# The order of 6,457 calls in an SSM and long-convolution kernel, written out anew

## The chip, the core and the metric

The kernel runs on one core of a Trainium2 chip. The metric is the device time of one execution in microseconds. The core has engines that run side by side, each with its own queue of instructions: PE (TensorE, matmuls, with PEld for its weight loads), DVE (VectorE), ACT (ScalarE), POOL (GpSimd) and SP (SyncE, which issues DMAs). An engine works through its queue in order, and an instruction that needs what another engine makes waits at the head of its queue, with all that stands behind it.

## The reference

Inputs are bf16, with a length of 2048, a width D of 448 and 256 modes per channel. Cut to what is computed:

```python
g = sigmoid((x * gate_w).sum(-1))
# branch A: a diagonal SSM; its kernel K has 2048 taps for each channel
P = exp(dt*A * l)                       # D x 256 x 2048, complex
K = einsum("dn,dnl,dn->dl", C, P, dt*B).real
a = irfft(rfft(x, 4096) * rfft(K, 4096))[:2048] + x * Dskip
# branch B: a shift of k by four taps, times v, then a convolution with ssm_k
kv = (four taps of k) * v
b = x * (irfft(rfft(kv, 4096) * rfft(ssm_k, 4096))[:2048] + kv * ssm_D)
out = g * a + (1 - g) * b
```

## The kernel before

The long convolutions are transforms in stages of matmuls. The 448 channels are cut into four quarters H (of each of 4 groups of 112 channels, 28); each of them is done for branch B and for branch A. A sequence is spread over frequencies by `spread` (matmuls with the table Wc into the PSUM tile ps_c), turned by `transform` (table W2, tile ps_2, which the profile calls ps), multiplied with the other factor's spectrum on DVE (`products`), and brought back by `stage_a` (table R, tile ps_a, result U) and `stage_b` (table G, tile ps_b). After each of these matmul groups the result is taken out of PSUM by a copy, nearly always on ACT ("evacuation"; CAST in the profile). There are three PSUM buffers for these groups. `swapped` makes a copy of a spectrum with its real and imaginary halves exchanged, by two DMAs (zsS<-zs).

The kernel K of branch A is made in eight blocks of 14 columns. `Tables.levels` and `Tables.reals` fill the table ET with powers: phases ks_ph on DVE, Sin and Exp on ACT (ACT has to load a table when it goes from one function set to another: ACT_TABLE_LOAD), products with magnitudes on DVE. `KGen.block` multiplies up two lists of powers, TQ (two buffers) and TP (one buffer), on DVE, and contracts them with up to 224 small matmuls into the one tile pk. ACT evacuates pk to kg_S, matmuls with a selection table gather it (ps_g) into kg_KT, and a spread brings it to zsK.

Other parts at the start: the tables Wc, W2, R and G are made from integer constants (POOL's iotas, small DVE operations in the tile scratch, Sin on ACT); the four taps of k are eight products kvt of DVE, summed by PE in ps_v with an identity matrix; the channel constants come from transposes ps_m of the loaded A, B and C ("modes"). The inputs are loaded by SP's queue. At the end, DVE weighs the last branch with the gate (tile ept), adds the rest (ug), and eight pairs of DMAs on SP and ACT store it.

The body is written once in program order, but nothing is issued there: `Order` only lists the calls (`Listed` stands in for each engine), 6,457 of them, numbered from 0. `Order.issue` then issues them as the string `ORDER` says, and ties each instruction to the one before it on its engine. The profile's line of nearly everything is L146 for that reason:

```python
for run in ORDER.split():
    a, _, b = run.partition("-")
    for f, args, kw in self.calls[int(a):int(b or a) + 1]:
        ins = f(*args, **kw)
```

A tile gets its buffer when it is first used in that order. The numbers that come up below:

| calls | what they are |
|---|---|
| 27 to 42; 43 to 48; 53 to 64 | SP's loads of k, of the modes, of v, ssm_k and u |
| 65, 73; 75, 74 | POOL's memset and iota; shift and identity made from it on DVE |
| 100, 110, 90, 120, 80, 130, 150, 140 | DVE: the products kvt, in the order of before |
| 234 to 241 | PE: transposes of one of the modes |
| 1463 | DVE: product that overwrites a spectrum, behind the DMA that reads it for its exchanged copy |
| 3996, 3997 | ACT Sin into ET; DVE product with its magnitude |
| 5398, 5399 | DVE: the two halves of a phase ks_ph |
| 5421, 5422; 5430, 5435, 5439 and 5431 | the same pairs for the last chunk of ET |
| 5446 to 5461 | ACT: the 16 Exp of the last chunk |
| 3681; 4427, 4428; 5196, 5197 | DVE: products of 128x3584, 2.02 us each |
| 3758, 3775, 3792 | ACT: evacuations of U from ps_a |
| 5084, 5125; 4810 | ACT: evacuations of a gather (kg_KT); of a transform |
| 5492; 5493 to 5716 | DVE: the last of block 6's TP; PE: its pk |
| 5879; 5880 to 6103 | DVE: the last of block 7's TP; PE: its pk, 224 matmuls |
| 5809 to 5824, 5827 to 5842 | PE: transform of zsK's first half (quarter 3), ps_2 |
| 5845 to 5848, 6271 to 6274 | DVE: products of 128x896 with the halves of zsK |
| 6105 to 6121, 6123 to 6162 | PE: the two gathers of block 7 |
| 5198 to 5256 | PE: ps_a groups (stage a of quarter 2) |
| 6164 to 6192; 6178, 6193 | PE: spread of block 7; its evacuations on ACT and DVE |
| 6205 to 6238 | PE: transform of zsK's second half |
| 6201, 6202 | DVE: the last mix of branches (uu, ug) |
| 6304; 6305 to 6452 | DVE: last evacuation of U; last stage b and its epilogue |

Of the kernel before, what the change touches and what calls it, by code (L numbers as in the profile page):

```python
# [41 lines left out]
    "604 23 166 27 73 65 26 31 576 1 75 164 525 74 24 36 76 171 194 192 172-173 198 193 25 35 188 177 174-175 195 582 "  # L42
    "189 580 176 0 34 199 581 201 162 593 160 33 163 594 161 190 165 595 588 167 2 168 577 32 597 178 169 606 602 29 "
    "22 16 191 17 179 21 12 38 13-14 18-19 15 181 186 10 28 180 182 8 170 20 9 3 187 6 183 37 11 7 5 4 30 536 534 528 "
    "526 184 42 79 68 529 185 527 46 535 39 537 544 47 542 196 545 531 197 44 550 202 200 590 583 552 45 543 541 584 "
    "596 589 48 585 591 100 40 530 41 55 533 43 586 101-108 592 603 587 72 67 599 598 49 110 51-52 538 66 90 50 56 "
    "234-241 69 77 532 54 120 53 109 64 242 70 63 215-222 78 80 539 62 243-250 71 540 225-232 61 223 549 224 233 "
    "121-128 130 548 203 546 204 131-138 150 129 547 111-118 551 139-140 600 151-158 119 553 601 554 251 141-148 159 "
    "557 252-259 267 149 319-326 260 327 302-317 556 285-300 318 261 91-98 301 262 555 205-212 81-88 213 99 214 263 "
    "268-283 264 89 265 1110 284 266 574 367 474 346-353 575 366 1111 472 578 471 481 1108 365 354 1109 476 502 473 "  # L50
    "607 364 470 469 468 475 494 561 579 570 565 573 558 566 559 517 563 516 569 478 518 490 512 503 507 498 477 513 "
    "487 489 479 482 519 491 608-635 493 480 483 492 495 486 484 387-402 488 499 496 500 508 1126 522 497 501 485 521 "
    "504 524 370-385 523 514 2488 505 509 636-663 515 506 510 664-691 520 1124 511 1113 692-719 386 1127 1115 1114 "
    "1116 560 421-428 1122 1117 1120 567 403 1129 1119 562 820-835 1131 571-572 1118 720 568 1112 564 429 1852 1121 "
    "721 803-818 2495 2510 2489 2499 2491 1133 2493-2494 2496 1123 2492 722 2490 1135 337-344 836 57 60 59 58 723 "
    "1125 2497 1141 404-419 819 724 345 725 355-362 2511 2498 1137 420 786-801 605 1128 363 777-784 1138 802 328-335 "
    "1130 1140 785 743-758 336 1132 430-437 1142 759-775 1134 1143 438 1464-1479 776 1136 457-464 1851 1139 1853 2500 "
    "1272-1335 1854 1862 837-844 1855 1857 1336-1367 465 1208-1271 2501 2503 2502 845 1856 2504 1480 369 368 2505 "
    "2520 1481-1496 2519 2512 1858 1515-1522 2521 960-967 1859 1144-1207 2506 2513 2523 1497 2514 2522 2515 1861 968 "
    "2524 448-455 1860 2516 439-446 1368 1864 1863 456 1369-1385 2517 2508 2507 2518 1865 969-976 1867 1386 447 1866 "  # L60
    "1387-1426 1869 977 1868 942-949 466 1427 726-741 950 1446-1451 2525 1498-1513 1870 742 2526 1848 1872 1514 1849 "
    "467 924-931 1847 932 906-913 1846 2509 1874 914 863-878 2542 2529 1877 2527-2528 897-904 2543 1523 1875 879-895 "
    "2545 1876 905 933-940 2530 2544 915-922 2563 896 2534 2531 2537 2562 2532 2538 1662-1669 923 2564 1850 2533 2565 "
    "941 1871 1644-1651 1670 1460 951-958 2566 1873 2535 846-861 1461 2569 1652 2536 1878 959 2202-2217 862 2568 1880 "
    "2218 978-1041 1879 2539 1452 1881 2555 2949-2964 1453-1458 2540 2074-2105 1463 2554 2556 2550 1043-1106 "
    "2557-2558 1462 2561 2546 2541 1882-1945 1459 2965 1107 2552-2553 2549 1042 2559 1437-1444 2551 1584-1599 2560 "
    "2573 1445 2567 2548 2966-2981 2547 1600 1428-1435 6194 3968 1618-1633 1436 2570 2982 1653-1660 2571 1946-2009 "
    "1661 2572 2574 1634 2010-2073 2577 3976 3994 3973 3988 1635-1642 3974 3987 3971 2576 2219-2234 2579 3975 2575 "
    "3977 3332 2581 1643 1601-1616 3995 3972 2583 3970 2106 2585 2578 1524-1539 2235 2588 2580 1617 3331 2125-2164 "
    "3333-3334 1575-1582 3969 2165 2582 1558-1573 1583 1540 3335 2107-2123 2584 1541-1556 1574 3337 1671-1678 2590 "  # L70
    "2124 2236-2251 1557 3338 2184-2189 1679 2589 1716-1779 2190 2199 3336 2252 2166-2173 2198 2591 3996 2983-2998 "
    "3339 1707-1714 1780 2174 3997 3000-3007 2999 3982 3341 2191-2196 3983 1715 2586 1698-1705 2197 2253-2260 3340 "
    "3008 3984 2587 1689-1696 1706 3343 2175-2182 2592 2261 1680-1687 1697 2322-2329 4008 3346 2785-2816 1688 "
    "2721-2784 4009 3348 2330 3985 3350 2183 2201 2593-2656 2200 2920-2927 2349-2356 2928 2657-2720 2357 3352 3354 "
    "3342 4010 2262-2277 3357 3345 2817 3344 4011 3989 3347 2818-2834 4012 2340-2347 4023 2278 4000 2313-2320 3999 "
    "4022 2348 3349 3156-3163 4024-4025 3351 2321 1781-1844 3164 4043 3353 4001 4014 2835 4013 2938-2945 4002 4015 "
    "3060-3067 3978-3979 2946 1845 2836-2875 3980 3043-3058 3990-3991 3068 3981 3992 4004 4016 2279-2294 3986 4003 "
    "3993 4005 4018 4042 2296-2311 3998 3355 3059 4044 3356 2295 2331-2338 3358 2312 3026-3041 4045 2876 3360 "
    "2929-2936 2339 2895-2900 4006 3361 4007 2909 3682-3697 2937 4017 4046 2910 4019 3359 2358-2421 4029 4047 "
    "3426-3489 4038 4020 4040 4050 4039 4037 2422 4021 4041 3362-3425 4030 4049 4031 3042 4048 3554-3585 4053 4052 "  # L80
    "4026 4034 4051 4032 4027 6197 4036 4033 2911-2918 4035 3490-3553 4028 4054 2919 5388 4057 3699-3714 3698 4812 "
    "2948 3733-3740 3586 3715 3138-3145 3741 2947 3129-3136 3146 3009-3024 5395 5390 3716-3731 5397 5402 5394 4056 "
    "5410 2901 5403 3025 4055 4059 2902-2907 4058 2908 4811 3174-3181 3732 4060 2886-2893 5411 4813 4062 5391 "
    "2423-2486 3137 4061 5393 5396 4064 5389 3811-3818 4063 2894 4069 3182 2877-2884 5392 2487 3069-3084 3819 4814 "
    "2885 3147-3154 3085 4070 3120-3127 3587-3603 3155 4815 3192-3199 4071 3604 4818 4446-4461 3200 4065 4820 "
    "3605-3644 5404 4068 4817 3103-3118 4066 3645 5399 3128 5398 3655-3662 4067 5400 3086-3101 5405 3663 4072 3119 "
    "3671-3676 5407 4265-4296 4816 3102 4732-4747 3677 5401 5412 4819 3802-3809 4748 5408 3646-3653 5414 4073-4136 "
    "4822 4821 5406 5413 4462 3678-3679 4823 3829-3836 4201-4264 5415 3654 4826 3837 6200 3165-3172 3664-3669 5416 "
    "4137-4200 4828 3810 5429 4830 3173 5428 5417 4832 5418 3183-3190 4824 4297 4825 4766-4773 4827 3191 3201-3264 "
    "4829 4774 3681 3670 5409 3820-3827 3265 5424 4298-4314 5423 4749-4764 3680 4315 5425 4463-4478 3828 4765 "  # L90
    "4316-4355 5426 4831 4409-4416 4479 3266-3329 5419 4833 4356 5420 4417 4839 5421 4838 5458 4480-4487 4382-4387 "
    "5422 4429-4444 4840 5457 5443 5427 5442 5459 5444-5445 3330 5463 5462 4835 4488 4391-4398 4388-4390 3793-3800 "
    "5455 5464 4836 4399 4357-4364 4834 5460 4841 4418-4425 5461 4445 4837 5473 5034-5065 5452 5465 5447 4842-4905 "
    "4426 6195 4970-5033 5448 5466 5454 5433 4365 5468 5456 5469 5451 5450 5467 5453 5446 5449 4375-4380 4400-4407 "
    "5430 5434 5470 4715-4730 6196 4906-4969 4408 5431 5437-5438 4731 5475 3759-3774 4428 4381 5066 5439 4366-4373 "
    "4802-4809 5476 5435 4427 4374 4810 5085-5124 5432 3776-3791 5125 5850 5472 3801 5471 3775 5067-5083 4549-4556 "
    "5436 5474 5084 4506-4521 5440 4557 5477-5478 5441 5151-5156 3742-3757 5479 3792 5480 5849 5482 5157 4567-4574 "
    "3758 5135-5142 5851 5484 4575 3838-3901 5486 4522 5490 5143 4540-4547 3902 4523-4538 5487 4548 5481 5144-5149 "
# [899 lines left out]
```

## Time and profile before

| what | us |
|---|---|
| median of 3 runs | 296.03 (294.1 to 296.98) |
| profiled execution | 296.28 |
| its span, first to last instruction | 293.9 |
| DVE idle in the span | 28.4 |
| ACT idle in the span | 39.6 |
| mean granted clock of PE | 0.874 |

The profile comes from one execution of the program. Its times count from the first instruction. A row of a timeline or a wait says in brackets how long the engine was idle before the instruction and what ended the wait. "Issue" is time in which an engine waited for nothing that the profile shows. The chain of waits is followed back from the last instruction to whatever released it.

### The profile page before, as it was taken

How to read it: one execution, taken by the hardware profiler on the slowest of the kernel's cores; microseconds unless marked ns; L12 is line 12 of the kernel's file. 1: busy time of each engine (PE TensorE's matmuls, PEld its weight loads, DVE VectorE, ACT ScalarE, POOL GpSimd, SP SyncE). 2: the span in 40 equal slices, each digit the busy share in tenths (PEclk: the TensorE clock that was granted, in tenths of full speed). 3: DMA queues.
4: the chain of work that ended last, by engine and by line, in shares of the span. 5: the costliest groups of instructions: out<-in, count | busy, mean ns of one | idle time of the engine just before them, and what ended most of it. 6: DMA issues, size and time to landing. Idle time of an engine off the chain costs nothing.

```text
span 293.9 us, 12044 instructions
## 1 busy us (share of the span) xinstructions
PE 214.2 (73%) x5387; PEld 186.9 (64%) x5387; DVE 265.5 (90%) x540; ACT 254.3 (87%) x411; POOL 9.4 (3%) x43
## 2 busy tenths in 40 slices
PE   0067771658866798997998688879687998689730
PEld 0043451547755688995888578769576897578730
DVE  8998999999999989898999999889999999795950
ACT  4999899999999998999799999989999997637500
POOL 7001100000000100000000000000000000000000
PEclk9995996755999895997999989989779999799965
DMA  7999999530234321023003310320500036000068
GB/s 129 189 189 150 164 156 265 104 58 0 46 85 65 62 68 49 4 51 79 4 2 65 76 41 3 64 68 6 125 4 2 4 79 161 19 6 4 2 113 141
DMA packets 53380, 21.34 MB, mean 73 GB/s; under 512 B 48720, under 2 KB 51664, under 8 KB 53328
## 3 DMA queue, kind: packets, MB, share of 16 engines
q1 hardware_dynamic: 48768, 19.42, 36.3%
q10 hardware_dynamic: 4560, 1.15, 2.3%
q8 instruction: 42, 0.69, 1.0%
q14 instruction: 10, 0.08, 0.1%
HBM read 10.01 MB, written 3.21 MB: 45 GB/s over the span
## 4 chain that ended last, share of the span: by engine, by line
ACT 49%; PE 20%; DVE 17%; issue 6%; SPq 2%; DMA 2%; DVEq 0%; ACTq 0%
ACT zs L146 15%; ACT ET L146 12%; ACT zsK L146 5%; PE ps_a L146 5%; ACT L146 4%; ACT U L146 4%; PE pk L146 4%; ACT ks_mag L146 3%; PE ps_b L146 3%; DVE kg_P L146 3%; PE ps L146 3%; PE ps_c L146 2%; SPq L146 2%; DVE kvt L146 2%; DVE zsS L146 2%
## 5 line engine op out<-in xcount | busy, mean ns | idle before, releaser
L146 ACT CAST zs<-ps 128x896 bf16<-128x896 f32 x48 | 44.7, 970 | 1.2 <-PE ps L146 1.2
L146 ACT CAST zs<-ps_c 128x1024 bf16<-128x1024 f32 (+1 forms) x48 | 44.1, 942 | 0.1
L146 PEld LDWEIGHTS <-s_W 128*128 128x128 bf16 x544 | 31.8, 106 | 16.7 <-issue 13.1
L146 PE MATMUL pk<-kg_TP,kg_TQ 128*25 128x32 bf16 x1792 | 32.5, 239 | 7.5 <-issue 7.2
L146 DVE TENSOR_TENSOR kg_P<-kg_TQ,ET 128x896 bf16<-128x896 bf16 (+2 forms) x56 | 36.4, 657 | 0.5
L146 PE MATMUL ps_a<-sa_R,zs 128*128 128x128 bf16 x224 | 34.3, 240 | 2.1 <-ACT zs L146 1.2
L146 PE MATMUL ps<-zs,s_W 128*128 128x112 bf16 x384 | 29.4, 228 | 7.4 <-ACT zs L146 5.7
L146 PEld LDWEIGHTS <-kg_TQ 128*25 128x25 bf16 x1792 | 28.1, 128 | 10.3 <-issue 8.5
L146 PE MATMUL ps_a<-sa_R,zsS 128*128 128x128 bf16 x224 | 33.6, 238 | 0.0
L146 PE MATMUL ps_b<-U,sb_G 128*128 128x28 bf16 x1024 | 28.3, 175 | 5.0 <-issue 2.0
L146 PEld LDWEIGHTS <-zsS 128*128 128x128 bf16 x224 | 30.2, 153 | 2.0 <-issue 1.7
L146 PEld LDWEIGHTS <-zs 128*128 128x128 bf16 x224 | 30.1, 152 | 1.9 <-DVE zs L146 0.5
L146 ACT CAST U<-ps_a 128x1024 bf16<-128x1024 f32 (+2 forms) x30 | 28.0, 964 | 3.8 <-PE ps_a L146 3.8
L146 PEld LDWEIGHTS <-sb_G 128*128 128x128 bf16 x1024 | 27.3, 96 | 6.0 <-issue 3.3
L146 DVE TENSOR_TENSOR kg_P<-kg_TP,ET 128x1792 bf16<-128x1792 bf16 (+1 forms) x32 | 31.0, 972 | 0.1
L146 PE MATMUL ps_v<-kvt,scratch 128*128 128x448 bf16 x64 | 16.1, 416 | 16.5 <-DVE kvt L146 14.1
L146 ACT ACTIVATE ET<-ks_ph 128x448 bf16<-128x448 int16 x40 | 23.2, 606 | 0.9 <-DVE kg_P L146 0.9
L146 DVE TENSOR_TENSOR kg_TQ<-kg_P 128x448 bf16<-128x448 bf16 (+2 forms) x56 | 23.5, 423 | 0.1
L146 PEld LDWEIGHTS <-scratch 128*128 128x128 bf16 x65 | 7.1, 112 | 24.0 <-issue 16.0
L146 PE MATMUL ps_c<-Wc,kv 128*64 128x128 bf16 x224 | 17.1, 310 | 7.1 <-ACT zs L146 6.5
L146 ACT CAST zsK<-ps_c 128x384 bf16<-128x384 f32 (+2 forms) x27 | 21.0, 779 | 0.2 <-PE ps_c L146 0.2
L146 DVE TENSOR_TENSOR kg_TP<-kg_P 128x896 bf16<-128x896 bf16 (+2 forms) x40 | 20.3, 507 | 0.9 <-PE pk L146 0.9
(103 smaller groups left out, 456.8 us busy)
## 6 DMA issues: line engine op xcount, KB each, us to landing
zsS<-zs SPq DMA_DIRECT2D x16, 448.0 KB, 5.4
kt<-in_B_k_dram SPq DMA_DIRECT2D x16, 112.0 KB, 4.1
vt<-in_B_v_dram SPq DMA_DIRECT2D x4, 448.0 KB, 6.9
skraw<-in_B_ssm_k_dram SPq DMA_DIRECT2D x16, 112.0 KB, 3.4
uu<-in_A_u_dram SPq DMA_DIRECT2D x4, 448.0 KB, 9.1
xfd<-ks_hold SPq DMA_DIRECT2D x2, 672.0 KB, 4.9
ks_xf<-xfd SPq DMA_DIRECT2D x3, 336.0 KB, 3.1
out_dram<-ug SPq DMA_DIRECT2D x8, 112.0 KB, 4.4
```

The lines of the kernel that those rows point to most:

```text
L146: ins = f(*args, **kw)
```

## The change

The calls, tiles and buffers are the same; the string `ORDER` is another permutation of the same 6,457 numbers. Every engine's order changes: the instructions of PE, DVE, ACT and POOL and the DMAs that SP and ACT issue. In the large it follows the same course. The 512 DVE calls up to call 5879 and its set are the same ones in both, in another order. On PE, 16 matmuls (5809 to 5824) go from ahead of pk of block 7 to behind it. On ACT, the Exps 5453, 5450 and 5449 go behind the last three Sins, which makes one more change of function set. On SP the loads at the start change places, the DMAs of an exchanged copy change within their pairs, and of the stores at the end the chunks come in another order. The lines of the string with the calls named above, of both orders:

```diff
--- before.py
+++ after.py
@@ -39,73 +39,74 @@
 NBH = 1
 
 ORDER = (
-    "604 23 166 27 73 65 26 31 576 1 75 164 525 74 24 36 76 171 194 192 172-173 198 193 25 35 188 177 174-175 195 582 "
...
-    "121-128 130 548 203 546 204 131-138 150 129 547 111-118 551 139-140 600 151-158 119 553 601 554 251 141-148 159 "
...
-    "2218 978-1041 1879 2539 1452 1881 2555 2949-2964 1453-1458 2540 2074-2105 1463 2554 2556 2550 1043-1106 "
...
-    "3339 1707-1714 1780 2174 3997 3000-3007 2999 3982 3341 2191-2196 3983 1715 2586 1698-1705 2197 2253-2260 3340 "
...
-    "3605-3644 5404 4068 4817 3103-3118 4066 3645 5399 3128 5398 3655-3662 4067 5400 3086-3101 5405 3663 4072 3119 "
...
-    "4426 6195 4970-5033 5448 5466 5454 5433 4365 5468 5456 5469 5451 5450 5467 5453 5446 5449 4375-4380 4400-4407 "
-    "5430 5434 5470 4715-4730 6196 4906-4969 4408 5431 5437-5438 4731 5475 3759-3774 4428 4381 5066 5439 4366-4373 "
...
-    "5436 5474 5084 4506-4521 5440 4557 5477-5478 5441 5151-5156 3742-3757 5479 3792 5480 5849 5482 5157 4567-4574 "
...
-    "5489 4576-4583 4539 3903-3966 5483 4584 5491 5485 5150 5492 4558-4565 3967 4784-4791 5126-5133 5852 4566 "
...
-    "5791 5876 5874 5792-5805 4714 5877 5169-5176 5806 5872 5878 5177 5809-5824 5875 5879 5826 5196 6072-6103 5825 "
-    "5944-6071 5197 5880-5943 6198-6199 5232-5247 6104-6121 5248 5807-5808 5846 5215-5230 5845 6122 5249-5256 5231 "
...
-    "5847-5848 6205-6220 6273 5322-5386 6222 6221 6274 6271 6241-6254 6272 5387 6201 6256-6269 6255 6202 6290-6303 "
...
+    "165 525 196 161 580 0 27 197 577 168 200 167 73 189 171 46 169 588 65 191 172 581 595 176 606 178 32 597 2 602 "
...
+    "531 52 56 90 533 53 70 540 54 215-222 62 120 109 67 77 539 71 225-232 64 78 223 63 538 111-118 224 61 150 233 "
...
+    "2557 2554 1453-1458 2558 2010-2073 2218 2966-2981 2556 2540 2549 1463 2949-2964 2561 2559 978-1041 2551 2555 "
...
+    "3000-3007 3995 2201 2657-2720 2348 3008 3996 4011 2313-2320 2817 3344 4000 3989 3999 2920-2927 3345 3997 4001 "
...
+    "4813 5392 5399 3147-3154 4814 3085 3120-3127 4066 2885 3103-3118 3155 4815 4067 3587-3603 3128 4820 3192-3199 "
...
+    "4399 4418-4425 4837 5467 5447 5034-5065 3792 4400-4407 5473 4970-5033 5470 4426 5469 3759-3774 4408 5437 6195 "
+    "5452 5446 5448 4428 5451 5430 4842-4905 3742-3757 4427 3775 4906-4969 3758 5433 4374 5431 5434 3838-3901 5432 "
+    "5438 5476 5435 5475 5850 5478 5439 5066 5472 4382-4387 5453 4540-4547 5480 5471 4523-4538 5436 5474 4388 5440 "
...
+    "5485 5491 4810 5490 4585-4648 5125 5852 5450 5449 5488 5151-5156 5853 4576-4583 4649 5492 5157 5855 5621-5684 "
...
+    "5944-6071 5197 5880-5943 6198-6199 5249-5256 6104 5232-5247 5257 5807-5808 6105-6121 5248 5198-5213 6122 "
+    "5215-5230 5214 6123-6162 5231 5827-5842 6163 5809-5824 5843 6179-6192 5844 5826 6193 6164-6177 5825 6178 "
...
+    "5258-5321 6255 6274 6273 6290-6303 5322 6275-6288 6201 6304 6289 6202 6343-6374 6305-6336 6375 6419-6450 6376 "
...
 )
```

## The prediction

> **What bounds the kernel now.** I read the busy row and the slices of the page first, then the sums by stretch, then the waits by engine, then the chain of waits in the tail, and last single rows of the timeline at the places where an engine idles.
>
> ```profile
> PE 214.2 (73%) x5387; PEld 186.9 (64%) x5387; DVE 265.5 (90%) x540; ACT 254.3 (87%) x411; POOL 9.4 (3%) x43
> 65.00:91.00 26.00, 20.58 (x535) 17.97 (x535) 25.83 (x62) 25.97 (x44) 0.00 (x0) 0.85 0.17 38
> 145.00:180.00 35.00, 28.61 (x745) 26.46 (x743) 34.50 (x74) 34.97 (x68) 0.00 (x0) 0.95 0.17 39
> 257.00:270.00 13.00, 10.96 (x413) 10.21 (x406) 8.76 (x9) 7.34 (x11) 0.00 (x0) 0.99 0.02 4
> 279.00:294.00 15.00, 3.10 (x122) 3.00 (x118) 4.07 (x8) 0.00 (x0) 0.00 (x0) 0.57 0.70 124
> ```
>
> The rows by stretch give the length, then PE, PEld, DVE, ACT and POOL busy. From 44 to 235 us DVE and ACT are both full: an order can move work there, but can only save an idle gap of both. After 255 us neither is full and the kernel is a chain of dependences; after 279 it drains to the store.
>
> No call is added or dropped, so durations stay and the whole question is idle time. DVE's last instruction before the tail is call 5879, the end of block 7's table of powers, which ends at 255.03. The same 512 DVE calls stand in front of it in both orders, 243.9 us of work, so 11.1 us are idle. These waits make up most of it, and ACT's own are as small:
>
> ```profile
> DVE kg_TP L146 <- PE pk L146: 1.8, 2, 0.9
> DVE kvt L146 <- PE ps_v L146: 0.9, 1, 0.9
> 106.86 2.02 DVE L146 TENSOR_TENSOR zs<-zs 128x3584 bf16<-128x3584 bf16 x1 [0.77 <-DMA zsS<-zs]
> 133.04 0.39 DVE L146 TENSOR_TENSOR ET<-ET,ks_mag 128x448 bf16<-128x448 bf16 x1 [0.86 <-ACT ET L146]
> 185.89 0.46 DVE L146 TENSOR_SCALAR ks_ph<-ks_xf 128x224 int32<-128x224 f32 x2 [0.75 <-ACT ET L146]
> 199.11 2.02 DVE L146 TENSOR_TENSOR zs<-zs 128x3584 bf16<-128x3584 bf16 x1 [0.36 <-ACT zs L146]
> 220.11 0.40 DVE L146 TENSOR_TENSOR ET<-ET,ks_mag 128x448 bf16<-128x448 bf16 x1 [0.63 <-ACT ET L146]
> 117.53 0.91 ACT L146 CAST zs<-ps 128x896 bf16<-128x896 f32 x1 [0.88 <-PE ps L146]
> 144.72 0.58 ACT L146 ACTIVATE ET<-ks_ph 128x448 bf16<-128x448 int16 x1 [0.88 <-DVE kg_P L146]
> ```
>
> **The method.** Every call is matched to its row by its place in its engine's order. For a call that waits on another engine I take its distance in the trace (its start less the producer's end), and add what the new order changes: busy time moved ahead of the waiting call, less busy time moved ahead of the producer. A gap goes if that sum is clearly positive; a wait comes, or grows, where it is negative.
>
> **The saturated stretch, to call 5879.** On DVE these gaps go: the tap product kvt at 27.96 (call 150 stands two products earlier, distance to its ACT evacuation still 1.2): 0.86. Call 3997 at 133.04 (2.36 to Sin 3996): 0.86. Call 1463 at 106.86, which waits for the swap DMA, has 3.0 us more DVE work ahead: 0.77. The phase 5399 at 185.89, now apart from its partner 5398: 0.75. Call 5431 at 220.11, now behind the two 2.02 us products 4428 and 4427 (1.89): 0.63. Call 3681 at 199.11 (0.39): 0.36. Sum 4.2 us. Waits that grow: the two on the single kg_TP buffer (0.55 and 0.32 more), its TQ partner 0.1, call 5422 behind Sin 5421 0.13, call 5492 behind Exp 5449 0.12; sum 1.2. DVE alone says -3.0 us.
>
> On ACT go 0.88 (117.53), 0.80 (142.13), 0.88 (144.72), 0.63 (32.87), 0.45 (31.34) and 0.32 (198.12): 4.0 us. But the new order makes one more table switch: Exp 5453 comes after the Sins 5430, 5435 and 5439, so after the run of Sin there is another of Exp, 14 loads for 13.
>
> ```profile
> 218.21 1.28 ACT L146 ACT_TABLE_LOAD   x1
> ```
>
> The first function behind such a load starts 1.31 us after the previous instruction ends (5430 at 219.50), so 1.3 us is the price. Here the Trainium skill speaks against the change: "ScalarE: Activation LUTs", section "What ACT_TABLE_LOAD costs", gives the same load but adds a drain, together about 2.66 us, and its rule is to do all calls of one set before switching. By the row ACT's sum is -4.0 + 1.3 = -2.7; by the rule -1.3. No row shows the drain, so I take 1.3.
>
> These sums are ceilings. The two engines feed each other, so a gap is saved only if both have the time, and ACT meets PE sooner in places: the three evacuations of U (calls 3792, 3775, 3758) were moved 8 to 13 us of ACT's work ahead, and against PE their distance becomes about -2 us if PE keeps its idle time (6.1 us between 205 and 235), nothing if PE's moved groups fill it. I take half of that, 1.1 us, as paid. So -2.7 + 1.1 = **-1.6 us at call 5879**, from -3.0 to +1.
>
> SP and POOL: the 16 loads of k, the six of A, B, C and the v and u loads change places in SP's queue. kvt 97, the first product, needs loads 31 to 34; the last is now eighth in the queue behind one 224 KB load, and eighth landed at 9.8; with about 1 us for the larger load it is 10.8. DVE gets there at about 13.6 (12.07 plus 1.6 us of small constants moved ahead): hidden, and about 3 us late before it costs. POOL's constants (iota 73 and memset 65) go behind the larger iotas, as the shift and identity that read them go later on DVE; PE starts at 14.13 anyway. The swap DMAs keep their order by pairs. The eight stores on each queue keep one per chunk.
>
> **The tail.** Rows:
>
> ```profile
> 253.93 1.10 DVE L146 TENSOR_TENSOR kg_TP<-kg_TP,ET 128x1792 bf16<-128x1792 bf16 x1
> 256.73 2.02 DVE L146 TENSOR_TENSOR zsS<-zsS,zsK 128x3584 bf16<-128x3584 bf16 x1 [1.70 <-ACT zsK L146]
> 255.97 0.91 PE ps L146 x16
> 256.87 2.56 PE pk L146 x135
> 259.43 1.37 issue
> 260.79 1.16 PE pk L146 x56
> ```
>
> (The last four are of the chain of waits: start, length, what.) Block 7's 224 matmuls could start at 255.1, but the transform 5809-5824 stands ahead of them and waits for ACT's zsK; they start at 256.80. The new order puts it behind: 1.7 us saved, and they end 5.25 us behind call 5879 instead of 6.92. Then it is given back. Two groups ps_a (0.67 and 1.23) stand ahead of the first gather and two of 1.23 ahead of the second, so the second gather ends 5.4 us behind pk, formerly 3.9. A DVE copy of 0.62 and the spread follow, which starts at about 11.75 behind 5879 (was 11.94). Behind it, ACT's zsK copy 6178 stands after four half copies (+0.5), the transforms 6205 and 6223 end 0.8 earlier, 1.2 us of products (5845, 5846) that filled a wait at 262.7 now lie in the busy part, and 6202 (1.09) leaves it, to run beside the last stage b. By rows the last stage b starts 11.55 behind the spread, formerly 11.70. Tail: **-0.3 us**, uncertain by 1.5. If the cover of 6202 fails (DVE late at the first addition) it costs up to its 1.09.
>
> **The issue waits.** PE waits 1.4 to 2.6 us "for nothing" in places such as 259.43. Counting matmuls, all six that are near 1 us or longer in pk, ps and ps_b without a late producer (at 166.41, 196.06, 216.94, 246.90, 252.27, 260.79) fall at numbers 128k+86 to 128k+88. The page's instruction queue moved 42 blocks of 16 KB in the span. The Trainium skill, "Runtime: NRT & Kernel Launch", section "Instruction fetch mechanics", says that code comes in blocks of 256 instructions (here 128 pairs of weight load and matmul), mostly hidden. The trace agrees on the spacing, not on the hiding. It matters because the boundary doesn't move with the order: number 4822 was the matmul 5881 of pk and is now 5897 of the same group. By the row I keep the 1.37 us in the tail; by the rule it would be gone and the forecast 1.4 lower. It is why no more than 1.7 is booked there.
>
> **The sum.** -1.6 - 0.3 = -1.9 on the profiled execution: 296.28 (its span 293.9 and 2.4 around it) to 294.4. It lies 0.25 above the median of 296.03; the runs spread from 294.1 to 296.98, more than the gain.
>
> **Rivals.**
>
> - *The gaps close fully* (0.25): DVE's -3.0 is reached and the U evacuations cost nothing, and a boundary misses pk: 296.3 - 3.0 - 0.3 - 1.4 = 291.6. For it: PE is idle 27% and the distances are positive. Against: the two kg_TP waits stay.
> - *A late Exp holds block 6* (0.20, slower). Exps 5450 and 5449 now stand on ACT behind two evacuations of gathers (5084, 5125) and a transform (4810); DVE's 5492, which ends block 6's TP, needs them, and pk of block 6 needs 5492. Distance -0.12 by busy time alone. It decides once PE brings the gather later than that: behind ACT are then all evacuations of U and zs, and a boundary wait (2.0 in the row of ps_b) on those gathers goes whole into the chain. Price 1.3 (load, now not covered) + 2.0 + 0.12, with none of the gains: 299.7.
> - *Nothing moves* (0.10): both engines full before and after, tail as worked out: 296.
>
> Forecast 0.45, its own range 293.0 to 296.2. About 1% is what a measurement of this kernel can tell from no change: below 293.1 is faster, above 299.0 slower. Faster: 0.25 of the first rival and 0.05 of the forecast; slower: 0.20. For 8 in 10 the range takes in most of the first rival and the lower half of the second: 290.6 to 299.2.
>
> **What would show it.** The waits of DVE for ACT ET and for the swap DMA shrink and those on pk stay near 1.8; 14 table loads; pk of block 7 starts within 0.3 us of call 5879, with the issue wait still in it; the second gather ends 5.4 us after pk. It would be wrong if call 5492 shows a wait for ACT of over 1 us, if ACT waits over 2 us for ps_a before 235, or if issue waits land on gathers in the tail.

## The result, and the profile after

| what | before | after |
|---|---|---|
| median of 20 runs each, us | 296.05 | 294.57 |
| lowest and highest, us | 294.1 and 298.34 | 291.22 and 298.04 |
| ratio to before, 95% interval | | 0.9925 [0.9895, 0.9954] |
| profiled execution and its span, us | 296.28, 293.9 | 294.42, 292.1 |

The kernel became 0.5 to 1.0% faster, 1.5 to 2 us; 294.4 was forecast. The ratios here and below leave out runs that are over 1.5% above the fastest of the same kernel, three of after's 20 and none of before's; over all 40 the ratio of the means is 0.9940. All lines of work are now L147, as `ORDER` is one line longer. The page's busy row of after:

```profile
PE 214.0 (73%) x5387; PEld 186.8 (64%) x5387; DVE 265.1 (91%) x540; ACT 255.3 (87%) x412; POOL 9.4 (3%) x43
```

The sums by stretch of after (length, then PE, PEld, DVE, ACT, POOL busy, the granted clock, DMA share, GB/s):

```profile
28.00:44.00 16.00, 12.80 (x119) 7.31 (x117) 13.11 (x15) 14.01 (x17) 1.83 (x1) 0.89 1.21 157
...
145.00:180.00 35.00, 29.02 (x766) 27.39 (x766) 34.93 (x72) 34.84 (x67) 0.00 (x0) 1.00 0.17 39
...
257.00:270.00 13.00, 11.82 (x319) 10.79 (x319) 6.64 (x11) 8.41 (x12) 0.00 (x0) 0.87 0.14 35
...
279.00:294.00 15.00, 1.52 (x59) 1.41 (x55) 3.19 (x7) 0.00 (x0) 0.00 (x0) 0.52 0.73 125
```

and the first of these stretches in the kernel before:

```profile
28.00:44.00 16.00, 12.97 (x128) 7.62 (x126) 15.34 (x16) 14.91 (x18) 1.93 (x1) 0.98 1.28 161
```

Work is the same to 1 us on every engine, so again only idle time has moved. The reader is to see three things: in this execution the front (28 to 44 us) got worse, DVE doing 2.2 us less work in it; the full stretches got a little fuller; and in the tail (257 to 270) PE's granted clock is 0.87 where it was 0.99. The waits of after (total us, times, longest) say where:

```profile
PE pk L147 <- issue: 4.3, 5, 1.4
ACT U L147 <- PE ps_a L147: 4.2, 4, 1.5
...
DVE ks_hold L147 <- PE ps_m L147: 2.9, 1, 2.9
...
DVE kg_TP L147 <- PE pk L147: 0.8, 1, 0.8
```

Single rows of after's timeline, first DVE, then ACT, then PE:

```profile
41.03 1.16 DVE L147 TENSOR_TENSOR ks_hold<-ps_m,ks_dt 128x448 f32<-128x448 bf16 x2 [2.86 <-PE ps_m L147]
...
222.98 1.28 ACT L147 ACT_TABLE_LOAD   x1
224.27 0.39 ACT L147 ACTIVATE ET<-ks_xf 128x224 bf16<-128x224 f32 x1
...
253.26 2.83 PE L147 MATMUL pk<-kg_TP,kg_TQ 128*25 128x32 bf16 x176 [1.85 <-DVE kg_TP L147]
257.54 0.92 PE L147 MATMUL pk<-kg_TP,kg_TQ 128*25 128x32 bf16 x48 [1.45 <-issue]
```

The course of the gain, as the end of a call in after less that in before: +1.1 us at call 264 (43.25; DVE, the front), +2.4 at call 1143 (78.08), -2.5 at call 3553 (165.98; PE), -1.8 at call 5879 (253.21), -1.5 at the last DVE instruction (282.69). So in these two executions the new order loses in the front, wins more than 4 us in the full stretches, gives some back before block 7, and gains nothing in the tail. How much of that belongs to the order and how much to the clock of the execution is a question to which the last experiments return.

### The profile page after: what moved, and what is told of

It is laid out like the page before. It is cut to its first block, busy times and chain, and to the rows that moved or that the text cites. A ratio compares the mean times of both kernels' runs of the same rounds, so it can differ in the third digit from the quotient of the medians.

```text
span 292.1 us, 12048 instructions
## 1 busy us (share of the span) xinstructions
PE 214.0 (73%) x5387; PEld 186.8 (64%) x5387; DVE 265.1 (91%) x540; ACT 255.3 (87%) x412; POOL 9.4 (3%) x43
## 3 DMA queue, kind: packets, MB, share of 16 engines
q10 hardware_dynamic: 4560, 1.15, 2.2%
## 5 line engine op out<-in xcount | busy, mean ns | idle before, releaser
L147 ACT CAST zs<-ps 128x896 bf16<-128x896 f32 x48 | 44.6, 955 | 0.8 <-PE ps L147 0.8
L147 ACT CAST zs<-ps_c 128x1024 bf16<-128x1024 f32 (+1 forms) x48 | 44.2, 946 | 0.1
L147 PEld LDWEIGHTS <-s_W 128*128 128x128 bf16 x544 | 31.7, 106 | 13.4 <-issue 9.8
L147 PE MATMUL pk<-kg_TP,kg_TQ 128*25 128x32 bf16 x1792 | 32.8, 239 | 7.2 <-issue 4.3
L147 DVE TENSOR_TENSOR kg_P<-kg_TQ,ET 128x896 bf16<-128x896 bf16 (+2 forms) x56 | 35.9, 650 | 0.2
L147 PE MATMUL ps<-zs,s_W 128*128 128x112 bf16 x384 | 29.0, 227 | 8.8 <-ACT zs L147 8.1
L147 PEld LDWEIGHTS <-kg_TQ 128*25 128x25 bf16 x1792 | 28.6, 128 | 9.9 <-issue 6.9
L147 PE MATMUL ps_a<-sa_R,zs 128*128 128x128 bf16 x224 | 33.6, 238 | 1.5 <-ACT U L147 0.7
L147 PE MATMUL ps_a<-sa_R,zsS 128*128 128x128 bf16 x224 | 32.8, 236 | 0.3 <-DVE zsS L147 0.3
L147 ACT CAST U<-ps_a 128x1024 bf16<-128x1024 f32 (+2 forms) x30 | 27.8, 952 | 4.4 <-PE ps_a L147 4.2
L147 DVE TENSOR_TENSOR kg_P<-kg_TP,ET 128x1792 bf16<-128x1792 bf16 (+1 forms) x32 | 30.8, 966 | 0.5 <-ACT ET L147 0.4
L147 PE MATMUL ps_b<-U,sb_G 128*128 128x28 bf16 x1024 | 28.2, 175 | 4.2 <-ACT U L147 2.0
L147 PEld LDWEIGHTS <-zsS 128*128 128x128 bf16 x224 | 30.0, 152 | 1.9 <-issue 1.2
L147 PEld LDWEIGHTS <-zs 128*128 128x128 bf16 x224 | 29.9, 152 | 1.6 <-DVE zs L147 0.3
L147 PEld LDWEIGHTS <-sb_G 128*128 128x128 bf16 x1024 | 27.7, 96 | 5.0 <-issue 3.1
L147 ACT ACTIVATE ET<-ks_ph 128x448 bf16<-128x448 int16 x40 | 23.4, 610 | 0.1
L147 DVE TENSOR_TENSOR kg_TQ<-kg_P 128x448 bf16<-128x448 bf16 (+2 forms) x56 | 23.2, 418 | 0.2
L147 PE MATMUL ps_v<-kvt,scratch 128*128 128x448 bf16 x64 | 17.6, 440 | 7.8 <-DVE kvt L147 6.0
L147 ACT CAST zsK<-ps_c 128x384 bf16<-128x384 f32 (+2 forms) x27 | 21.3, 795 | 1.3 <-PE ps_c L147 1.2
L147 PE MATMUL ps_c<-Wc,kv 128*64 128x128 bf16 x224 | 17.2, 307 | 5.4 <-ACT zs L147 4.6
L147 DVE TENSOR_TENSOR kg_TP<-kg_P 128x896 bf16<-128x896 bf16 (+2 forms) x40 | 20.0, 500 | 0.8 <-PE pk L147 0.8
```

## The experiments

Each kernel is the changed kernel with the edit shown. A list `CALLS` holds the numbers of `ORDER`, and `move(order, what, ahead_of)` puts some of them elsewhere. The ratio is to the kernel before on the same chip. The times within the span come from one profiled execution each, so a difference of 1 or 2 us between two rows need not come from the edit. e0 is the changed kernel with nothing moved, measured together with e3b, e4 and e5; over all 12 of its runs its mean is 0.9983 of before's. "In pk" is PE's wait without a visible cause in pk of block 7; the last column is the time from the end of call 5879 to the last DVE instruction.

| run | ratio, 95% interval | call 264 ends | call 5879 ends | in pk | tail |
|---|---|---|---|---|---|
| before | | 42.11 | 255.03 | 1.37 | 29.16 |
| after | 0.9925 [0.9895, 0.9954] | 43.25 | 253.21 | 1.45 | 29.48 |
| e0_control | 0.9964 [0.9933, 0.9994] | 42.91 | 254.39 | 1.14 | 29.36 |
| e1_front_new | 0.9907 [0.9869, 0.9944] | 43.03 | 254.25 | 1.35 | 29.02 |
| e2_tail_new | 1.0036 [1.0009, 1.0063] | 42.95 | 255.78 | 0.94 | 28.78 |
| e3_exp_early | 0.9922 [0.9891, 0.9952] | 41.59 | 251.63 | 1.79 | 29.95 |
| e3b_three_exps_early | 0.9926 [0.9896, 0.9956] | 41.59 | 250.84 | 3.13 | 31.25 |
| e4_gathers_first | 0.9958 [0.9922, 0.9993] | 41.68 | 251.86 | 3.19 | 32.30 |
| e5_shift_64 | 1.0103 [1.0068, 1.0138] | 41.58 | 254.03 | none | 30.29 |
| e6_evac_first | 0.9986 [0.9954, 1.0018] | 40.83 | 253.62 | 1.62 | 29.89 |
| e9_swap_late | 0.9886 [0.9846, 0.9927] | 41.59 | 250.74 | 0.91 | 28.01 |
| e10_old_tail_swap_late | 1.0008 [0.9978, 1.0038] | 41.58 | 250.69 | 1.00 | 31.68 |
| e11_gathers_swap_late | 0.9908 [0.9876, 0.994] | 41.58 | 250.94 | 1.14 | 29.73 |
| e12_fill | 0.9924 [0.9902, 0.9946] | 42.61 | 253.63 | 0.76 | 27.92 |

### Which half gains: the order up to pk, or the tail

```diff
+OTHER = numbers(BEFORE)
+FIRST = set(CALLS[:CALLS.index(6072)])
+CALLS = [i for i in CALLS if i in FIRST] + [i for i in OTHER if i not in FIRST]   # e1_front_new
+CALLS = [i for i in OTHER if i in FIRST] + [i for i in CALLS if i not in FIRST]   # e2_tail_new
```

> The new order up to the point where block 7's pk begins, and from there the order of before, with the transform 5809-5824 ahead of pk again. My theory: the gain is made in the saturated stretch, where call 5879 ends 1.8 us earlier, and the new tail is worth about nothing; so about 1.5 to 2.2 us under the kernel before, 294.0 to 294.6. The rival (starting pk at once is what gains, and the stretch ahead of it only shifts idle time): within 0.5 us of before, about 296.

> The order of before up to block 7's pk, and from there the new order: pk at once, the transform behind it. My theory: pk starts about 1.7 us earlier behind call 5879, the second gather ends later behind pk by about that, and the end is within 0.5 us of before, about 296. The rival (pk first is the gain): about 1.7 us under before, 294.3.

The new front with the old tail has the gain (0.9907, 2.7 us, more than the 1.5 to 2.2 expected); the old front with the new tail is 0.4% slower than before (1.0036), 0.8 to 1.1 us where within 0.5 was expected. So the gain is made ahead of pk, and the new tail by itself brings none in the times. In e2's profile the tail was 0.4 us shorter (28.78 for 29.16), and pk did start 0.2 us behind call 5879, for 1.8 in before; why its times are above before is not settled.

### The fourteenth table load

```diff
+CALLS = move(CALLS, [5453], 5430)               # e3_exp_early
+CALLS = move(CALLS, [5450, 5449, 5453], 5430)   # e3b_three_exps_early
```

> The new order with one call moved: Exp 5453 goes ahead of Sin 5430, so 13 table loads for 14. If the load is paid in full on the way to call 5879: 1.3 us faster than the changed kernel, 1.28 us less of ACT's busy time and call 5879 about 1 us earlier. If it lies in time in which ACT would have waited anyway: within 0.4 us of the changed kernel. If a load also drains the pipeline as the Trainium skill has it: 2.6 us faster.

This expectation rested on a slip: three Exps stand behind the Sins, and with one of them moved the load only went on to the next. The profile of e3 still has 14.

> The changed kernel with all three late Exps (5450, 5449, 5453) ahead of Sin 5430, so that the 14th table load really goes (the run with 5453 alone only moved it on to 233 us, since the other two stayed). If the load is paid in full: call 5879 about 1.3 us earlier and 1.3 us faster. If it is covered by ACT's waits for PE: within 0.4 us. If a drain belongs to it: 2.6 us faster.

Here it goes. The groups of instructions of e3b (busy us, mean ns, then idle time ahead):

```profile
L165 ACT ACT_TABLE_LOAD x13 | 16.7, 1283 | 4.2 <-DMA kt<-in_B_k_dram 4.0
```

Call 5879 ends at 250.84, against 251.86 in e4, whose order is that of after up to there and whose front was as early: 1.0 us. It is the wait of call 5492 for the late Exp 5449 that went. DVE's rows of 5492 in e0, and then in e3b:

```profile
236.84 1.09 DVE L165 TENSOR_TENSOR kg_TP<-kg_TP,ET 128x1792 bf16<-128x1792 bf16 x1 [1.14 <-ACT ET L165]
...
233.30 1.08 DVE L165 TENSOR_TENSOR kg_TP<-kg_TP,ET 128x1792 bf16<-128x1792 bf16 x1
```

In e4 that wait was 1.12 us, and 1.07 in e3, where the load stands right ahead of the late Exps. The edit takes away a load and brings the Exps forward at once, so the 1.0 us is what both are worth together; the load's part is not separated. No switch shows a drain: the next function starts 1.30 to 1.31 us after the instruction ahead of the load at every switch in before and after. The kernel is not faster than the control clear of noise (0.9926 against 0.9964, intervals overlapping), and in the tail of its profile the gain was lost: its timeline on PE has

```profile
250.89 2.88 PE L165 MATMUL pk<-kg_TP,kg_TQ 128*25 128x32 bf16 x176 [1.91 <-DVE kg_TP L165]
256.90 0.91 PE L165 MATMUL pk<-kg_TP,kg_TQ 128*25 128x32 bf16 x48 [3.13 <-issue]
```

### The waits for nothing that the profile shows

```diff
+            if n == 608:            # in PE's wait of 5.9 us for the gate's tile; overwritten later
+                jobs = [(self.tc.nc.tensor.matmul, (self.pg[:, 256:272],),
+                         dict(lhsT=self.R[:, 0:128], rhs=self.R[:, 0:16], start=True, stop=True))] * 64 + jobs
```

> The changed kernel with 64 matmuls more on PE, put where PE waits 5.9 us for the gate's tile (their result is overwritten), so that every later matmul's number is 64 higher. If the issue waits belong to fixed numbers (128k+86 to 128k+88): they all move to other instructions, at numbers that are 128k+22 to 128k+24 by the old count; the 1.45 us inside block 7's pk goes or moves by 64 matmuls, and the end comes 0 to 1.4 us earlier. If they belong to the instructions (the change of group, the PSUM tile, DVE or ACT traffic): they stay at matmul 4821 of the old count and the time is unchanged.

They belong to the numbers. Counted in its own stream, e5's waits lie at 128k+86 to 128k+90, as those of all other runs do (up to 128k+91 in before and e2), that is 64 matmuls earlier in the work. Its timeline shows pk of block 7 in one piece, and a wait later:

```profile
254.09 3.57 PE L169 MATMUL pk<-kg_TP,kg_TQ 128*25 128x32 bf16 x224 [1.13 <-DVE kg_TP L169]
...
260.99 0.28 PE L169 MATMUL ps_a<-sa_R,zs 128*128 128x128 bf16 x1 [1.53 <-issue]
```

The time was a miss: not 0 to 1.4 us earlier, but some 3 us later than the control (297.45 against 294.5). Its waits say why:

```profile
PE pk L169 <- issue: 6.7, 6, 2.1
DVE kg_TP L169 <- PE pk L169: 2.9, 3, 1.9
```

With the boundaries elsewhere, the pk groups of other blocks are hit harder, and DVE then waits for the single kg_TP. The same pair of rows fits part of the change's own gain: in before they were 7.2 and 1.8 us, in after 4.3 and 0.8. The prediction had left that out; how much of the gain it makes is not measured.

What a wait consists of can be read from the records of the instruction queue. In after PE takes matmul 4694 (the boundary ahead) at 253.98; a 16 KB packet runs from 254.62 to 256.07; PE goes on at 257.54. From passing one boundary to going on at the next it takes 3.1 to 3.6 us at this place in after, before, e0, e1 and e2, while 128 matmuls of pk take about 2.0 (224 of them took 3.57 us above). In e3b the packet starts 2.9 us behind the boundary (251.61, 254.53) instead of 0.6. Two rows by stretch show the DMA share in the 2.9 us from the boundary in e3b, and in the 2.9 us from the start of the packet in after:

```profile
251.60:254.50 2.90, 2.17 (x144) 2.01 (x133) 2.90 (x2) 0.00 (x0) 0.00 (x0) 1.00 0.84 168
```

```profile
254.60:257.50 2.90, 1.50 (x100) 1.37 (x90) 2.90 (x3) 0.00 (x0) 0.00 (x0) 1.00 1.02 228
```

What moves there is the last exchanged copy, 896 KB, issued by SP when its source and buffer come free: 5808 is issued by 252.13 in e3b and 254.55 in after, each about 0.6 us behind the boundary, and the copy moves in both stretches (DMA share 0.84 and 1.02). In before it had been issued by 246.36, far from this pk. The new order brings copy and fetch together. In after, e0, e1 and e6 the fetch starts beside the copy, 0.55 to 0.64 us behind the boundary, and the wait in pk is 1.1 to 1.6 us; in e3 it starts 1.51 behind, in e3b and e4 2.9, and the wait is 1.8 and 3.1 to 3.2. What decides between the two is open: the distance from copy to boundary is not it, as SP's second issue starts 0.08 us ahead of the boundary in e0 and e3b alike, and 0.11 in e6 and e4 alike. e9 takes the copy away from there:

```diff
+CALLS = move(CALLS, [5450, 5449, 5453], 5430)
+CALLS = move(CALLS, [6104, 5807, 5808], 6105)
 ...
+                if n in (5807, 5808):
+                    f = self.tc.nc.scalar.dma_start
```

> The changed kernel with the three Exps early (as before) and with the last exchanged copy's two DMAs (5807, 5808) issued by ACT behind 6104 instead of by SP, so that they move after block 7's pk and not during it. My theory (the fetch of the next 128 matmuls is asked for when PE enters a block, and stands behind the exchanged copy's 896 KB if that is already under way): PE's wait inside this pk falls from 3.13 us to 1.0 to 1.5 us, and the end comes about 1.7 us earlier than with the Exps alone. The rival (the long wait comes from where the pk stands in time, or from DVE and ACT): it stays near 3.1 us. If the copies then land too late, DVE's 5847 waits for them at about 267 us.

Its timeline, PE and then ACT's queue:

```profile
250.79 2.85 PE L168 MATMUL pk<-kg_TP,kg_TQ 128*25 128x32 bf16 x176 [1.50 <-DVE kg_TP L168]
254.55 0.92 PE L168 MATMUL pk<-kg_TP,kg_TQ 128*25 128x32 bf16 x48 [0.91 <-issue]
...
256.17 0.51 ACTq L168 DMA_DIRECT2D zsS<-zs  x1
256.71 0.61 ACTq L168 DMA_DIRECT2D zsS<-zs  x1
```

0.91 us for 3.13, and the copy comes in time for 5847 at 263.59. No profile without the copy near has a long wait: in the six whose copy is not near this pk (before, e2, e9 to e12) it is 0.76 to 1.37 us, in the seven where it is (after, e0, e1, e3, e3b, e4, e6) 1.14 to 3.19, in three of them over 1.7. With one profile for each kernel that fits the theory, and is not yet proof of it. (The move also puts 6104 on ACT behind the evacuation 5257, so ACT's copy of pk starts 1.2 us behind the end of pk.) The tail is 3.2 us shorter than in e3b, more than the 2.2 us of the wait. The rest goes with the clock: e3b has half clock from 257.0 to 260.4, e9 none there. With 0.9886, 291.52 us, e9 has the lowest ratio here: its interval lies below 1, and the ratio also below the changed kernel's (0.9925 and 0.9964 in two measurements; only the first of these intervals overlaps its own). Against e3b (0.9926) the intervals overlap, so the 1.7 us expected from the copy alone are not shown in the times.

### The tail's order

```diff
+TAIL = ("5232-5247 6104-6121 5248 5215-5230 6122 5249-5256 5231 6123-6162 5257 "
+        "5198-5213 6163 5214 6179-6193 6164-6178 5827-5844 5809-5826")
+CALLS = move(CALLS, numbers(TAIL), 5323)        # e4; e11 has e9's two moves besides
```

> The changed kernel with another order of the tail: only one group of ps_a ahead of block 7's first gather, the gathers as early as PE can take them, the transform 5809-5824 behind the spread. My theory (what the early start of pk gained is given back because the gathers wait behind two ps_a groups each): the second gather ends about 1.5 us earlier behind pk and the kernel ends about 1 us earlier than the changed kernel. The rival (the tail is bound by ACT's and DVE's copies and by the clock of PE there, so order doesn't matter): within 0.4 us of the changed kernel.

> The tail with the gathers first, now with the three Exps early and the exchanged copy late, so that the wait of 3.19 us in pk, which hid its effect, is out of the way. My theory (gathers behind two groups of ps_a each gave the early pk back): the wait is 1.0 to 1.5 us, the second gather ends about 1 us sooner behind pk than with the tail as changed, and the kernel ends about 0.5 to 1 us before the run with the copy late alone. The rival (copies on ACT and DVE and the half clock behind pk bound the tail): the same time within 0.4 us.

No gain is shown. From the end of pk to the end of the second gather it took 5.6 us in e4 (6.3 in e0), but the wait of 3.19 us ate that. In e11 that wait is gone, and the gather comes 5.1 us behind pk, just as in e9, and the ratio is above e9's (0.9908, intervals overlapping). Two things went against it: the issue of the copy's DMAs held ACT, and DVE's product 5848 waited for ACT's zsK, because I had put the transform 5809-5824 behind the spread (timeline of e11, ACT and then DVE):

```profile
256.03 2.85 ACTq L171 DMA_DIRECT2D zsS<-zs  x2
258.92 1.01 ACT L171 CAST U<-ps_a 128x1024 bf16<-128x1024 f32 x1 [2.44 <-PE ps_a L171]
...
265.18 0.63 DVE L171 TENSOR_TENSOR zs<-zs,zsK 128x896 bf16<-128x896 bf16 x1 [1.31 <-ACT zsK L171]
```

(The second row names PE, but its group of ps_a had ended by 257.1; ACT went on when the DMA issues were through.) So my theory that the gathers' place gave the early pk back is not supported; its effect with nothing else moved stays open.

> New order up to block 7's pk, the tail of before behind it, the three Exps early and the last exchanged copy late. If the parts add up: the new front with the old tail was 0.9907 of before, the Exps are worth about 1 us at call 5879, and the wait in pk stays near 1.3 us: about 0.987 of before, 291 us. If the old tail only gains because its DVE waits less, the Exps' gain is lost in the wait for the transform ahead of pk: about 0.990.

Its edit is e1's lines with e9's two moves. A miss (1.0008). The old tail had DVE's products 5846 and 5845 ahead of the gather's copy 6163, and the late copy now makes them wait (DVE timeline of e10):

```profile
262.16 0.63 DVE L241 TENSOR_TENSOR zs<-zs,zsK 128x896 bf16<-128x896 bf16 x1 [5.47 <-DMA zsS<-zs]
```

So e10 tests only this collision, not whether the parts add up.

### The wait in the front

```diff
+CALLS = move(CALLS, [556, 557, 554], 555)       # e6_evac_first
```

> The new order with three Sins of table G (554, 556, 557) moved on ACT behind the evacuations that follow them at 33 to 43 us. My theory: DVE's new wait of 2.86 us at 41.03 (ks_hold for the transposes ps_m, whose PSUM buffer ACT frees late) goes, and since DVE is 99% busy for the 200 us that follow, most of it reaches call 5879: 1.5 to 2 us faster than the changed kernel, about 292.8. The rival: the front is bound by ACT and PE as well, and the Sins come back as a wait of ACT or DVE before 110 us; within 0.5 us of the changed kernel.

No gain, as the rival had it: 0.9986, if anything slower than the changed kernel. DVE's wait at 41 us went (call 264 ends at 40.83), but the Sins come behind: ACT's first Exp (call 472) starts at 45.47, against 44.10 in e4, whose front ran at full clock as this one did, and DVE waits 1.15 us for ET at 53.63. Call 5879 ends at 253.62, not earlier than in after.

But e0, e1, e3, e3b and e4 have the front of after unchanged, and call 264 ends at 42.9 to 43.0 in the first two and at 41.6 to 41.7 in the others. Sums over two stretches of 3.41 us of after show the difference:

```profile
33.90:37.31 3.41, 1.68 (x41) 1.33 (x41) 3.38 (x4) 3.41 (x5) 0.00 (x0) 1.00 1.33 161
37.31:40.73 3.42, 3.42 (x15) 1.65 (x14) 0.85 (x1) 2.63 (x4) 0.00 (x0) 0.51 0.85 139
```

and of e4:

```profile
34.80:38.20 3.40, 1.91 (x29) 1.32 (x29) 3.37 (x3) 3.40 (x5) 0.00 (x0) 1.00 1.26 151
38.20:41.60 3.40, 3.30 (x37) 1.95 (x36) 2.39 (x6) 2.97 (x5) 0.00 (x0) 1.00 0.98 159
```

The same part of the work runs at half clock in after (0.51) and at full clock in e4. The clock records change only at steps of 3.41 us, whose phase differs from one execution to the next. I tabulated all such steps between 60 and 278 us of 13 profiles, by PE's busy share in one step and the clock granted in the next, where the step itself was at full clock (a step that lies on the edge of a class can fall to either side):

```
busy share   next at half clock   next at full clock
under 0.5            40                   0
0.5 to 0.6           14                  13
0.6 to 0.7           12                  51
0.7 to 0.8           11                 107
0.8 to 0.9            3                 148
over 0.9              0                 295
```

Under half and over 0.9 the share tells what comes; between 0.5 and 0.8 both outcomes occur, so it is not the whole rule. The changed front sits on the edge: a share of 0.49 in after, 0.52 in e0 (half clock follows), 0.56 in e4 (full). Where it falls under, call 264 is 1.3 to 1.7 us late and is not made up: call 5879 ends 1.4 us later in after than in e4, and 2.4 to 2.5 in e1 and e0, with the same order up to there. So the loss in the front was of that execution: at full clock the changed front brings call 264 to 41.6 us, before's to 42.11, and e2, with the front of before, ended it at 42.95. The tail is alike. Rows of after:

```profile
255.73:259.14 3.41, 1.96 (x84) 1.75 (x74) 3.38 (x3) 0.53 (x1) 0.00 (x0) 1.00 0.79 186
259.14:262.56 3.42, 3.42 (x44) 2.94 (x43) 0.07 (x1) 2.04 (x3) 0.00 (x0) 0.50 0.01 2
```

The wait of 1.45 us in pk makes the first step 57% busy, and the next, with the gathers in it, runs at half clock. In e9 the corresponding steps are fuller, and the clock stays at 1.00:

```profile
253.05:256.47 3.42, 2.51 (x105) 2.26 (x94) 3.38 (x3) 0.31 (x1) 0.00 (x0) 1.00 0.02 5
256.47:259.88 3.41, 3.32 (x60) 3.09 (x58) 0.27 (x1) 3.00 (x5) 0.00 (x0) 1.00 0.79 168
```

The last run tried to lift the front over the edge:

```diff
+FILL = {285: 20, 91: 20, 608: 88}   # matmuls of 64 columns ahead of these calls, overwritten later; on top of e9
```

> The run with the Exps early and the last exchanged copy late, plus 128 small matmuls whose result is overwritten: 20 ahead of the spread at 35 us and 20 ahead of the sum at 37 us, where PE waits 0.8 and 0.7 us, and 88 in PE's 5.9 us wait for the gate's tile; 128 in all, so that the block boundaries behind them stay where they are. My theory (the clock of each stretch of 3.41 us is halved when PE was busy less than about 55% of the stretch before; the changed kernel sits at 0.49 to 0.56 there, and where it falls under, the front is 1.7 us late and stays so to the end): PE's share there rises to 0.7 or more, call 264 ends at 41.6 us, no half clock begins at 37 to 38 us in any execution, and the times lose their upper part: 0.3 to 0.8 us less in the median than the same kernel without the fill (0.9886 of before), about 0.986. The rival (half clock in the front comes at random, or the extra matmuls only delay PE): the same or up to 1 us slower, with the same spread.

Partly right. The share rose to 0.66, not 0.7. Rows of e12:

```profile
34.80:38.20 3.40, 2.24 (x62) 1.99 (x62) 3.37 (x3) 3.40 (x5) 0.00 (x0) 1.00 1.32 160
38.20:41.60 3.40, 2.80 (x29) 1.68 (x26) 1.45 (x4) 2.44 (x4) 0.00 (x0) 1.00 0.93 151
41.60:45.00 3.40, 2.06 (x33) 1.35 (x32) 3.40 (x8) 2.32 (x3) 0.00 (x0) 1.00 1.34 156
45.00:48.45 3.45, 2.65 (x90) 2.53 (x87) 3.45 (x6) 3.44 (x9) 0.00 (x0) 1.00 1.42 178
```

and of e9 without the fill:

```profile
41.42:44.83 3.41, 0.56 (x8) 0.40 (x8) 3.41 (x7) 3.38 (x6) 0.00 (x0) 1.00 1.35 161
44.83:48.25 3.42, 0.00 (x0) 0.00 (x0) 3.42 (x5) 3.42 (x12) 0.00 (x0) 0.50 1.32 223
```

In e9 PE was busy 16% of the step from 41.4 us, and half clock followed, from 44.8 to 55.1; with the added work (which also makes the work behind it come later) it was busy 61% and 77% of the steps from 41.6 and 45.0, and the clock stays full until 51.8. So the clock followed a share that an edit had changed. The times lie closer (292.19 to 293.42, six runs; e9 290.66 to 292.97, six runs). But a group of 20 took 0.75 us, as long as the wait it was to fill, and held up what came behind: the sum after it starts at 38.28 instead of 37.25, call 264 ends 1.0 us later, and by its ratio (0.9924) the kernel is slower than e9, the intervals overlapping. That no execution has half clock at 37 to 38 us can't be seen from one profile.

## Why the prediction was right, by its steps

- **DVE's gaps.** Of the six that were to go (4.2 us), five went or shrank to under 0.3; that of 5399 (0.75) stands with the same size at another phase, call 5410, and a wait of 0.53 for an exchanged copy is new (call 2200). But two terms were missing, and they offset each other. The pair of waits on kg_TP was to grow by 0.9; it fell from 1.8 to 0.8, as PE's boundary waits in pk fell from 7.2 to 4.3. And a wait of 2.86 us (1.0 to 1.1 in executions with a full clock there) arose at 41 us: the small constants moved ahead of the taps, which I took as hidden, had been DVE's cover while PE made the transposes. With the front late, DVE's idle time ahead of 5879 fell by 1.6 us (11.1 to 9.5), not 3.0; in e4, with the front early, it was 8.0.
- **The table load.** Priced at 1.3 by the row; removing it and bringing the Exps forward brought 1.0 at call 5879. The page "ScalarE: Activation LUTs" of the Trainium skill ("What ACT_TABLE_LOAD costs") would have had 2.66; no run shows the drain. Its rule ("Table sets: the hidden batching unit"), all calls of a set before the switch, was right in direction: e3b follows it and ends the stretch earlier.
- **The evacuations of U.** ACT's waits for ps_a ahead of 235 us are 0.13 us in after; the rest of their 4.2 us lies behind 259. The 1.1 booked did not come.
- **SP and POOL.** Hidden, as said: kvt of call 100 starts at 13.74 (13.6 worked out).
- **The sum at call 5879.** -1.6 forecast, -1.8 in the profile. That they agree so closely is luck. Terms of opposite sign, each larger than the error, were missing; and other executions of the same order end the call 0.6 us (e0), 0.8 us (e1) and 3.2 us (e4, front early) ahead of the one profile of before. The last is where the rival that all gaps close had put it.
- **The tail.** pk starts 0.05 us behind 5879, and ACT takes its result 5.3 us behind it (5.25 worked out for pk's end). The second gather, set at 10.65 (5.4 behind pk), ended at 11.41 (6.2): this is the mis-sized term. It was counted by rows at full clock, and PE ran at half clock from 259.14 to 262.56; in e2, where the same tail's gathers ran at full clock, the gather came 5.49 behind pk and the tail was 0.4 shorter than before's. In after the spread came at 12.27 for 11.75, and from 5879 to DVE's end it took 29.48 us, formerly 29.16: +0.3 for -0.3.
- **The issue waits.** Right in place (matmul 4822 within pk) and size (1.45 for 1.37). What I did not see is that a reorder can bring a copy to them, that the longest of them (1.8 to 3.2) were seen only with a copy under way, and that half clock can follow them.
- **The late Exp.** Call 5492 did wait for ACT, 0.62 us in after and 1.07 to 1.15 in e0, e1, e3 and e4. Over 1 us was named as a sign of being wrong, and by these executions it was met: the 0.12 booked was too little. The mechanism of the slower rival is real, and too small to turn the sign.

## What to carry to other kernels

In a stream of small matmuls, count where each block of 128 weight-load and matmul pairs ends, and try keeping large DMAs away from the moment at which the next block is fetched; a reorder that saves a wait on an engine may move a copy there. When two engines are full, judge a moved instruction by the wait that it used to cover. And compare profiles of one kernel with each other before explaining 1 or 2 us between two kernels: look at the granted clock by stretches of 3.41 us first.

## What the runs showed of the hardware

- PE's clock changes by steps of 3.41 us and goes with the busy share of the step before: under half, a step at full clock was always followed by one at half clock (40 of 40); over 0.9, never (0 of 295); between, both occur. The Trainium skill ("TensorE: Matmul & The Clock Gate", "What's actually happening") states the free-running window of this length; the shares, and that a step with one wait of 1.45 us in it can be enough, are of these runs. The phase differs from execution to execution, and one unchanged front ended 1.3 to 1.7 us apart.
- From one block boundary of PE to going on at the next, in block 7's pk, it took 2.9 to 3.5 us in the six profiles without the copy of 896 KB near, and 3.3 to 5.3 in the seven with it; the packet itself is 16 KB and took 0.9 to 1.7 us there. The same skill's "Runtime: NRT & Kernel Launch" ("Instruction fetch mechanics") calls the crossing mostly hidden; here PE waited 4.3 us at it in pk in after and 7.2 in before.
- The same two DMA issues took ACT's queue 0.51 and 0.61 us in e9, 1.39 us together in e10 and 2.85 us in e11. Why is open.
